# Moving the reciprocals of softmax sums from ScalarE's Ln and Exp to a power on GpSimd

## The chip, the cores and the metric

The kernel runs on one core of one Trainium2 chip. The metric is the time of one execution on the device, in microseconds (us); lower is better. Inside the core, PE (TensorE) does the matrix products, ACT (ScalarE), DVE (VectorE) and POOL (GpSimd) do elementwise work, SP issues DMAs. Each engine works through its own list of instructions in order and waits for semaphores where an instruction needs another engine's result.

## The reference

Attention with a softmax that has one more term in its denominator, followed by a feed-forward block with squared relu. There are 8 batches, 12 heads, 448 positions and a head dimension of 64; the block has 3584 tokens, width 768 and inner width 2048.

```python
def _attn_ref(q, k, v):
    scale = 1.0 / np.sqrt(q.shape[-1])
    scores = scale * np.matmul(q, k.transpose(0, 1, 3, 2))
    m = np.max(scores, axis=-1, keepdims=True)
    e = np.exp(scores - m)
    attn = e / (np.sum(e, axis=-1, keepdims=True) + np.exp(-m) + 1e-09)
    return np.matmul(attn, v)
# x = attention's output as [8 * 448, 12 * 64]
def _moe_ref(x, w_in, w_out):
    h = x @ w_in
    r = np.maximum(h, 0.0)
    return (r * r) @ w_out
```

Without the subtraction of the maximum the weights are exp(s) / (sum of exp(s) + 1). The kernel computes that form, so it needs one reciprocal of (sum + 1) for each query and head.

## The kernel before, in words

The twelve heads of a batch are worked on as three quads of four heads. Batches 1 to 7 give 21 quads, numbered m = 0 to 20 (three to a batch); batch 0 is worked on in halves by functions of its own and is not touched by the change. A quad goes through these steps, each a letter in a written-out list of steps:

- `s` (`quad_scores`): scores of 64 keys at a time into a PSUM tile `sp`; `e` (`quad_exp`, recorded at L254): ScalarE's exp of it, to a tile `et` or `nn`. There are seven of each to a quad.
- `a` (`add_quad`, L441 to L447): VectorE adds the exps of the seven pieces, in four instructions, to `half`.
- `S` (`sums_of_quad`): four matmuls with `ones`, whose entries are 1/256 (`GS` is 256), sum over the keys; each sum lands, already repeated over 64 rows, in a PSUM tile `zp`, of the kind `sp`.
- `Z` (`quad_z`, L463): ScalarE reads `zp` (128 x 896) and writes ln(sum/256 + 1/256) to an SBUF tile `rcp`; the 1/256 comes in as the bias `one_b`.
- `M` (`quad_reciprocal`, L466): ScalarE's exp(-x) in place, which is 256/(sum + 1).
- `v` (`values_step`): 28 matmuls of the exps with the values, into two PSUM tiles `mp`.
- `X` (`quad_x`, L487): two VectorE multiplies of `mp` and `rcp`, to the block's input `xt`.

The feed-forward block uses the letters `j` (matmuls with `win`), `k` (`relu`, L503 on ScalarE or L505 on VectorE), `l` (`squared`, L509, to `gs`), `o` (`out_piece`, matmuls with `wout`), `O` and `Q` (`out_first` and `out_second`, L575, L577 and L581, which evict the output; `store` then sends it from SP's queue). `d` issues loads: weights (`load_win`, `load_wout`), values (`load_v_quads`), staging of the queries and keys of later batches in DRAM (`stage`), transposed loads from there (on SP), and `tail_keys` (L188), copies by GpSimd that wait for those. All of GpSimd's loads and copies are in one queue.

The order is written by hand, as two strings, `ORDER` for the start and `CYCLE` for pairs of batches from the fourth on. Every engine's list follows that order, so a step that moves to another engine stands in that engine's list where its letter stands in the string. For instance, near the end of `ORDER`:

```
... Z7 Q12 a8,2 o13,12,16 v7,0 v7,1 v7,2 v7,3 O13,1 v7,4 a8,3 v7,5 v7,6 M7 S8 Q13 v8,0 v8,1 Z8 v8,2 v8,3 M8 v8,4 v8,5 X7 v8,6 X8
```

PSUM holds two `sp` tiles of two banks and, after the start, a ring of four `mp` tiles of one bank. Every `v`, `j` and `o` takes its tiles from that ring: a quad's values take two and give them back at `X`, a tile of the output takes two and gives them back at `Q`, a tile of the hidden layer takes one and gives it back at `k`. `z_pool` has two `rcp` tiles.

Of the kernel before, what the change touches and what calls it, by code (L numbers as in the profile page):

```python
# [9 lines left out]
FP32 = mybir.dt.float32  # L10
FP16 = mybir.dt.float16
AF = mybir.ActivationFunctionType
ALU = mybir.AluOpType
# [3 lines left out]
def kernel(  # L17
# [9 lines left out]
    nc = tc.nc  # L27

    B, H, S, D = q.shape
# [12 lines left out]
    scale = 1.0 / float(D) ** 0.5  # L42
    GS = 256.0
# [4 lines left out]
    consts = ctx.enter_context(tc.tile_pool(name="consts", bufs=1))  # L48
# [340 lines left out]
    eqs, esq, zqs = {}, {}, {}  # L389
# [70 lines left out]
    def quad_z(m):  # L460
        zp = zps.pop(m)
        rcp = zqs[m] = z_pool.tile([128, 2, S], FP32, name="rcp")
        nc.scalar.activation(out=rcp, in_=zp[:, :, 0:S], func=AF.Ln, bias=one_b)  # L463

    def quad_reciprocal(m):
        nc.scalar.activation(out=zqs[m], in_=zqs[m], func=AF.Exp, scale=-1.0)  # L466

    xqs = {}

# [120 lines left out]
    idle = nc.const_aps.tensor(1.0, [128, 512], mybir.dt.bfloat16)  # L590
    ones = consts.tile([128, 64], FP16)
    nc.vector.memset(ones, 1.0 / GS)
    one_b = consts.tile([128, 1], FP32)
    nc.vector.memset(one_b, 1.0 / GS)
    raw = load_first_quad()
# [38 lines left out]
    def quad_visit(n):  # L634
# [25 lines left out]
        "a": lambda m, step: add_quad(m, step),  # L660
        "S": lambda m: sums_of_quad(m),
        "Z": lambda m: quad_z(m),
        "M": lambda m: quad_reciprocal(m),
        "v": lambda m, c: values_step(m, c),
        "X": lambda m: quad_x(m),
# [46 lines left out]
    def period(b):  # L712
# [16 lines left out]
        def block(n):  # L729
# [5 lines left out]
            "a": lambda x, step: add_quad(m + x, step),  # L735
            "S": lambda x: sums_of_quad(m + x),
            "Z": lambda x: quad_z(m + x),
            "M": lambda x: quad_reciprocal(m + x),
            "v": lambda x, c: values_step(m + x, c),
            "X": lambda x: quad_x(m + x),  # L740
# [85 lines left out]
```

## Time and profile before

| | before |
|---|---|
| median of 2 runs | 392.89 us (391.95 to 393.84) |
| the profiled execution | 393.06 us |
| its span (first to last instruction) | 391.3 us |
| PE busy | 383.2 us, 98% |
| DVE busy | 251.9 us, 64% |
| ACT busy | 228.5 us, 58% |
| POOL busy | 62.2 us, 16% |

The profile is of one execution. Its span is 1.8 us shorter than the time of that execution; what lies around the span is not in any row. A row of a group gives the line, the engine, the operation, the tiles written and read, their shape, how many instructions there were, their busy time in us and the mean of one in ns, then the idle time of the engine just before them and what ended it. In a timeline a row begins with the start and the duration in us. GpSimd's spans in a profile are rough. The granted TensorE clock was 1.00 over all stages of this execution.

Three parts can be told apart in the order of time: up to about 47 us loads and batch 0; to 318 us attention and feed-forward work interleaved, with PE busy in nearly all of it (89.4 of 90 us from 47 to 137, and 45.0 of 45 from 183 to 228); after 318 us feed-forward work alone. The 21 logarithms of line L463 start between 47.8 and 314.3 us.

### The profile page before, as it was taken

The page shows a single profiled execution, that of the slowest core. Times are in us where ns is not written, and L with a number is a line of the kernel's source. Part 1 is how long each engine was busy: PE and PEld are TensorE (multiplying, and loading weights), DVE is VectorE, ACT ScalarE, POOL GpSimd, SP SyncE. Part 2 cuts the span into 40 slices and gives each one's busy share as a digit, 9 for nine tenths or more (in the row PEclk, how much of TensorE's full clock was granted, in tenths as well). Part 3 has the DMA queues.
Part 4 walks back from the last instruction along what each step waited for, and adds up shares of the span by engine and source line. Part 5 has one row for each costly group of instructions (what it writes and reads, how often), then busy time and mean ns, then how long its engine had stood idle before and what let it go on. Part 6 is the DMA issues. An engine that isn't in the chain of part 4 may idle for free.

```text
span 391.3 us, 14259 instructions
## 1 busy us (share of the span) xinstructions
PE 383.2 (98%) x6432; PEld 253.7 (65%) x6432; DVE 251.9 (64%) x468; ACT 228.5 (58%) x308; POOL 62.2 (16%) x96
## 2 busy tenths in 40 slices
PE   9789999999999999999999999999999999999997
PEld 5566656565789755667777665667777755556665
DVE  2887995765666766556968757566778788880000
ACT  5999998586689511349988731248988730001221
POOL 8544420025000701300001240310000000000000
PEclk9999999999999999999999999999999999999999
DMA  8999999999939899903129596941112200001132
GB/s 143 203 205 205 202 203 205 182 182 175 215 75 175 158 195 149 160 2 66 44 54 194 145 182 131 151 46 44 52 55 64 64 23 2 0 0 61 62 82 80
DMA packets 75052, 45.34 MB, mean 116 GB/s; under 512 B 47472, under 2 KB 72944, under 8 KB 74992
## 3 DMA queue, kind: packets, MB, share of 16 engines
q0 software_dynamic: 24752, 22.62, 37.4%
q1 hardware_dynamic: 49952, 21.59, 28.1%
q8 instruction: 50, 0.82, 0.9%
q10 hardware_dynamic: 288, 0.23, 0.2%
q14 instruction: 10, 0.08, 0.1%
HBM read 45.69 MB, written 17.93 MB: 163 GB/s over the span
## 4 chain that ended last, share of the span: by engine, by line
PE 86%; ACT 6%; DMA 2%; SPq 2%; DVE 1%; issue 1%; POOL 1%; ACTq 0%; POOLq 0%; DVEq 0%
PE mp L93 77%; PE sp L93 8%; ACT et L254 4%; SPq L166 2%; DMA nn<-in_k_dram 2%; PE mp L207 1%; DMA out_dram<-ot 1%; ACT rcp L372 1%; ACT nn L254 0%; DVE qk L217 0%; ACT rcp L365 0%; ACT ot L575 0%; DVE half L341 0%; ACT rcp L463 0%; DVE half L447 0%
## 5 line engine op out<-in xcount | busy, mean ns | idle before, releaser
L93 PE MATMUL mp<-wout,gs 64*64 64x384 f16 (+2 forms) x2928 | 165.2, 322 | 0.0
L93 PE MATMUL mp<-xt,win 128*64 128x448 f16 (+2 forms) x1188 | 148.3, 347 | 0.1
L93 PEld LDWEIGHTS <-gs 64*64 64x64 f16 (+1 forms) x2928 | 103.1, 106 | 34.5
L93 PEld LDWEIGHTS <-win 128*64 128x64 f16 (+1 forms) x1188 | 83.2, 106 | 63.5 <-issue 4.2
L254 ACT ACTIVATE et<-sp 128x896 f16<-128x896 f32 (+2 forms) x131 | 110.6, 889 | 12.3 <-PE sp L93 11.7
L505 DVE TENSOR_SCALAR rt<-mp 128x448 f16<-128x448 f32 x87 | 54.1, 622 | 17.4 <-PE mp L93 14.5
L509 DVE TENSOR_TENSOR gs<-rt 128x448 f16<-128x448 f16 x128 | 47.8, 390 | 22.1 <-ACT rt L503 20.2
L503 ACT ACTIVATE rt<-mp 128x448 f16<-128x448 f32 x41 | 21.8, 543 | 65.0 <-PE mp L93 55.7
L575 ACT ACTIVATE ot<-mp 128x384 f32<-128x384 f32 (+2 forms) x31 | 14.9, 480 | 71.6 <-PE mp L93 68.8
L93 PE MATMUL sp<-qk 64*64 64x224 f16 (+1 forms) x1056 | 53.7, 274 | 2.1 <-DVE qk L217 0.5
L93 PEld LDWEIGHTS <-qk 64*64 64x64 f16 x1056 | 32.7, 115 | 15.2 <-issue 6.5
L188 POOL COPY flatq<-qk 64x384 f16<-64x384 f16 x20 | 14.8, 739 | 172.7 <-DMA qk<-stage_k 126.0
L254 ACT ACTIVATE nn<-sp 128x896 f16<-128x896 f32 x42 | 37.1, 916 | 4.3 <-PE sp L93 4.2
L487 DVE TENSOR_TENSOR xt<-mp,rcp 128x448 f16<-128x448 f32 x42 | 24.2, 619 | 15.7 <-ACT rcp L466 10.3
L581 DVE SCALAR_TENSOR_TENSOR ot<-mp,ot 128x384 f32<-128x384 f32 x42 | 23.4, 556 | 15.3 <-ACT ot L575 12.4
L93 PEld LDWEIGHTS <-vn 64*64 64x64 f16 x756 | 22.4, 107 | 10.4 <-issue 1.8
L93 PE MATMUL mp<-et,vn 64*64 64x448 f16 (+1 forms) x448 | 24.5, 343 | 0.0
L577 DVE TENSOR_SCALAR ot<-mp 128x384 f32<-128x384 f32 x26 | 14.4, 555 | 14.3 <-PE mp L93 14.2
L463 ACT ACTIVATE rcp<-sp,one_b 128x896 f32<-128x896 f32 x21 | 21.1, 1007 | 2.8 <-PE sp L93 2.7
L466 ACT ACTIVATE rcp<-rcp 128x896 f32<-128x896 f32 x21 | 19.9, 949 | 0.5
L441 DVE TENSOR_TENSOR half<-et 128x1792 f16<-128x1792 f16 x15 | 16.3, 1088 | 4.3 <-ACT et L254 4.2
L443 DVE TENSOR_TENSOR half<-half,et 128x1792 f16<-128x1792 f16 x15 | 16.3, 1086 | 0.3
(59 smaller groups left out, 197.4 us busy)
## 6 DMA issues: line engine op xcount, KB each, us to landing
out_dram<-ot SPq DMA_DIRECT2D x52, 96.0 KB, 2.9
out_dram<-ot SPq DMA_DIRECT2D x19, 192.0 KB, 1.9
win<-in_moe_w_in_dram POOLq DMA_DIRECT2D x8, 384.0 KB, 12.3
wout<-in_moe_w_out_dram POOLq DMA_DIRECT2D x4, 768.0 KB, 14.9
vn<-in_v_dram POOLq DMA_DIRECT2D x10, 288.0 KB, 8.4
stage_q<-in_q_dram POOLq DMA_DIRECT2D x4, 676.0 KB, 13.1
stage_k<-in_k_dram POOLq DMA_DIRECT2D x4, 676.0 KB, 15.9
nn<-in_q_dram POOLq DMA_DIRECT2D x8, 224.0 KB, 8.6
```

The costliest lines, as they stand in the source:

```text
L93: return nc.tensor.matmul(out_, lhsT, rhs, start=start, stop=stop)
L254: nc.scalar.activation(out=out_, in_=in_, func=AF.Exp, scale=scale)
L441: nc.vector.tensor_add(esq[m], a[:, 0:w], a[:, w:2 * w])
L443: nc.vector.tensor_add(esq[m], esq[m], z[:, 0:w])
L463: nc.scalar.activation(out=rcp, in_=zp[:, :, 0:S], func=AF.Ln, bias=one_b)
L466: nc.scalar.activation(out=zqs[m], in_=zqs[m], func=AF.Exp, scale=-1.0)
L487: nc.vector.tensor_mul(xts[b][:, 2 * g + i, :], xqs[m][i][:, 0:S], zqs[m][:, i, :])
L503: nc.scalar.activation(out=rt[:, 0:m], in_=hp[:, 0:m], func=AF.Relu)
L505: nc.vector.tensor_scalar(out=rt[:, 0:m], in0=hp[:, 0:m], scalar1=0.0, scalar2=None, op0=ALU.max)
L509: nc.vector.tensor_mul(gs[:, f0:f0 + per, t0 % RING:t0 % RING + n], r, r)
L575: nc.scalar.activation(out=ot, in_=op[:, 0:w], func=AF.Copy, scale=OUT_SCALE)
L581: nc.vector.scalar_tensor_tensor(out=ot, in0=lo[:, 0:w], scalar=OUT_SCALE, in1=ot, op0=ALU.mult, op1=ALU.add)
```

## The change

For the quads of batches 1 to 7, `Z` becomes a VectorE addition of 1/256 that reads the sums from PSUM and writes them to `rcp`, and `M` becomes a GpSimd instruction with two tensors as inputs that raises `rcp` to the power of a tile `minus`, filled with -1 by GpSimd at the start. Batch 0 keeps ScalarE's Ln and Exp. The strings of the order are the same.

```diff
     def quad_z(m):
         zp = zps.pop(m)
         rcp = zqs[m] = z_pool.tile([128, 2, S], FP32, name="rcp")
-        nc.scalar.activation(out=rcp, in_=zp[:, :, 0:S], func=AF.Ln, bias=one_b)
+        nc.vector.tensor_scalar(out=rcp, in0=zp[:, :, 0:S], scalar1=1.0 / GS, scalar2=None, op0=ALU.add)
 
     def quad_reciprocal(m):
-        nc.scalar.activation(out=zqs[m], in_=zqs[m], func=AF.Exp, scale=-1.0)
+        nc.gpsimd.tensor_tensor(out=zqs[m], in0=zqs[m], in1=minus, op=ALU.pow)
...
     ones = consts.tile([128, 64], FP16)
     nc.vector.memset(ones, 1.0 / GS)
+    minus = consts.tile([128, 2, S], FP32)
+    nc.gpsimd.memset(minus, -1.0)
     one_b = consts.tile([128, 1], FP32)
```

In the built program the 21 additions stand in VectorE's list and the 21 powers in GpSimd's. The memset of `minus` (128 x 896) stands in GpSimd's list ahead of its first loads. The powers of quads 0 to 2 stand between loads of values and of `wout` and the first staging loads, that of quad 3 behind the four copies of batch 3's `tail_keys`.

## What was predicted

> **What bounds the kernel now.** I read the page first: busy times, then the chain that ended last.
>
> ```profile
> span 391.3 us, 14259 instructions
> PE 383.2 (98%) x6432; PEld 253.7 (65%) x6432; DVE 251.9 (64%) x468; ACT 228.5 (58%) x308; POOL 62.2 (16%) x96
> PE 86%; ACT 6%; DMA 2%; SPq 2%; DVE 1%; issue 1%; POOL 1%; ACTq 0%; POOLq 0%; DVEq 0%
> ```
>
> PE is busy for 383.2 of 391.3 us and makes up 86% of the chain. Only 8.1 us of PE idle time exist, so relieving ScalarE, here or anywhere, can win at most 2%; whatever makes PE wait is paid in full. The question is therefore how late the normalized rows (`xt`) come, and how long PE can go on without them.
>
> Then the groups by line, for the instructions that the change touches or that I price it by:
>
> ```profile
> L463 ACT ACTIVATE rcp<-sp,one_b 128x896 f32<-128x896 f32 x21 | 21.1, 1007 | 2.8 <-PE sp L93 2.7
> L466 ACT ACTIVATE rcp<-rcp 128x896 f32<-128x896 f32 x21 | 19.9, 949 | 0.5
> L487 DVE TENSOR_TENSOR xt<-mp,rcp 128x448 f16<-128x448 f32 x42 | 24.2, 619 | 15.7 <-ACT rcp L466 10.3 <-PE sp L93 3.8 <-PE mp L93 1.7
> L505 DVE TENSOR_SCALAR rt<-mp 128x448 f16<-128x448 f32 x87 | 54.1, 622 | 17.4 <-PE mp L93 14.5
> L577 DVE TENSOR_SCALAR ot<-mp 128x384 f32<-128x384 f32 x26 | 14.4, 555 | 14.3 <-PE mp L93 14.2
> masks.py:199 POOL TENSOR_SCALAR_AFFINE_SELECT ident<-ident 128x128 f16<-128x128 f16 x1 | 0.3, 288 | 0.1
> ```
>
> The 21 logarithms (L463) and 21 exponentials (L466) take 1.007 and 0.949 us each. The multiply that uses them (L487) already waits for them, 10.3 us in all, without cost to PE: there is some cover, but it has been tested over about 1 us at a time only.
>
> Then the timeline of ScalarE, VectorE and GpSimd around single quads (start, duration):
>
> ```profile
> 80.45 1.00 ACT L463 ACTIVATE rcp<-sp,one_b 128x896 f32<-128x896 f32 x1
> 81.48 0.95 ACT L466 ACTIVATE rcp<-rcp 128x896 f32<-128x896 f32 x1
> 82.46 1.16 DVE L487 TENSOR_TENSOR xt<-mp,rcp 128x448 f16<-128x448 f32 x2 [2.00 <-ACT rcp L466]
> ...
> 82.02 1.29 POOL L188 COPY flatq<-qk 64x384 f16<-64x384 f16 x2 [30.35 <-DMA qk<-stage_k]
> 86.31 1.82 POOL L188 COPY flatq<-qk 64x384 f16<-64x384 f16 x2 [3.01 <-DMA qk<-stage_k]
> ```
>
> From the start of the logarithm to the multiply are 2.01 us; in 12 of the 21 quads it is 2.0 to 2.1. GpSimd, which now gets the second step, spends its queue waiting for transposed loads there: these copies stand ahead of this quad's power in program order.
>
> **The change part by part.** ScalarE loses 42 instructions, 41.0 us; by the 8.1 us above this is worth little. On the one stretch where they are on the chain (116.43 to 118.12 us) they are 1.67 us; I count this gain as nothing and keep it for a rival.
>
> VectorE gains 21 additions of 128x896 from PSUM. L577 and L505 give 555 ns for 384 columns and 622 for 448, that is 1.05 ns a column, so 622 + 448 x 1.05 = 1.09 us, against 1.007 on ScalarE.
>
> GpSimd gains 21 powers of 128x896 f32. No row shows a power. Its nearest row of price is the select above, 288 ns for 128 columns, 2.25 ns a column: one simple pass over 896 is 2.0 us, the lower bound. A power of two tensors is a logarithm, a product and an exponential; if each is a polynomial with its splitting and scaling, I estimate 16 steps, and a pass of 2.0 us for each step gives 32 us, the upper bound. Steps in one loop needn't load and store each time, yet sixteen can't be free as in a table: I take the geometric middle, 8.0 us, and keep both ends.
>
> The Trainium skill's GPSIMD Engine Reference, section 3.1, has bodies of more than two operations run at about 3 operations a cycle of 1.2 GHz; with some 48 operations that is an estimate of 12 us, and the sum below would end near 618. No run here shows that rule.
>
> Now the delay of one quad. Addition 1.09, power 8.0, one more handover 0.1, less the 2.02 of before: the multiply can start 7.17 us later. VectorE is in order, and the multiply waits at the head of it: relu (L505), squares (L509), sums of exps (L441 to L447) and the output's evictions (L577, L581) queue behind it, and PE waits for these, since the ring of PSUM tiles holds four and the values of the quad keep two until the multiply.
> - 21 quads: 21 x 7.17 = 150.6.
> - Five quads (7/8, 10/11, 13/14, 16/17, 19/20 as pairs) issue the second addition ahead of the first multiply. There the second multiply follows the first after one power, 8.0, where it now follows after 2.1: it adds 5.9, not 7.17. 5 x -1.27 = -6.4.
> - Queue of GpSimd: the copies end at 88.13 (86.31 + 1.82) where the addition would end at 81.54: +6.6 for quad 3. The copies at 222.22 + 1.52 = 223.74 stand ahead of quad 12's power, ready at 218.15: +5.6. Together 12.2. The weight and staging loads behind the first three powers move by some us each; the first use of the second half of `wout` is near 81 us against a landing at 67 to 77, so I count nothing, and if that cover is gone the loads cost what the powers ahead of them do, which is in the 7.17 already.
> - The memset of 128x896 on GpSimd ahead of its first loads, which open the chain: between 0.1 (a 128x1 memset) and 2.0 (the pass above); I take 1.0.
> - Cover: behind the values PE has one output tile that needs no VectorE, 64 matmuls of 64x384; 32 of them take 1.30 us in the chain, so 2.6. VectorE must afterwards catch up two multiplies and an eviction, 2 x 0.62 + 0.56 = 1.8. That leaves 0.8 a quad: -16.8.
>
> Sum: 150.6 - 6.4 + 12.2 + 1.0 - 16.8 = +140.6. The profiled execution took 393.06 (span 391.3 and 1.8 around it), 0.2 above the median 392.89. 393.06 + 140.6 = 533.7, say 534.
>
> **The rivals.**
> Cheap power. At 2.0 us the delay of a quad is 1.17: 24.6 - 6.4 + 12.2 + 1.0 - 16.8 = +14.6, 408; without cover, because VectorE is 70 to 90% busy in those slices, 424. For it: every GpSimd row is near 2 ns a column. Against: none of them computes a function.
> Dear power. At 32 us: delay 31.17; 654.6 - 6.4 + 12.2 + 1.0 - 16.8 = +644.6, 1038. For it: nothing but the step count; against: steps in registers cost less than passes.
> Port. A power that reads SBUF holds off VectorE's additions of two SBUF tensors, so one L441 (1.08 us) of each quad that now runs before the multiply starts after the power: 21 x 1.08 = 22.7, 534 + 22.7 = 556. For it, by the groups of single lines:
>
> ```profile
> L188 POOL COPY flatq<-qk x20: 609/624/1360, 82.0 to 258.7; 64x384 f16<-64x384 f16 x20
> L509 DVE TENSOR_TENSOR gs<-rt x128: 376/391/601, 30.4 to 352.7; 128x448 f16<-128x448 f16 x128
> ```
>
> The same copy takes 609 to 1360 ns and the same square 376 to 601; something holds them. Against: in a quad that waits for the power VectorE has little else to do. The Trainium skill's SBUF page (SBUF — State Buffer, section "SBUF: two separate sides") calls the pair of ports that VectorE and GpSimd share an exclusive lock for a whole instruction; the longest copies here agree with it.
> Not slower. If the power took under 1.6 us (0.83 that the new steps may cost, and the 0.8 of cover), as the fastest copy's 609 ns for 384 columns, 1.4 us for 896, would allow, every multiply would come in time. ScalarE's exps, freed of 1.67 us on the chain, would repay the memset, and with the copies (12.2) hidden by PE's order the time would be 393.06 - 1.67 + 1.0 = 392.4. Against: the 12.2 has no visible cover, and the copy has one input and no arithmetic.
> That GpSimd does not get the work is excluded: in the built order 21 powers stand on its queue and 21 additions on VectorE's.
>
> **How the numbers follow.** Forecast, a power of about 4 to 16 us without further loss: 0.45. Cheap 0.22, dear 0.18, port 0.08, not slower 0.07. The range runs from the cheap power with a short memset (393.06 + 13.7 = 407, taken as 405) to the dear one (1038, taken as 1040); outside lie the last rival and a power slower than the passes. Within 2% (385 to 401, about what a measurement of this kernel tells from no change) is the last rival and nearly nothing else, 0.07; faster by more than 2% would need all of PE's idle time, 0.01; slower 0.92.
>
> **What would show each step.** Right: a group on POOL of 21 instructions near 8 us; VectorE's waits headed by the multiply for GpSimd's `rcp`, near 21 x 6 us; PE's share of the span near 72% (383 of 532); the power of quad 3 held by the copies. ScalarE's busy time near 188. Wrong: a power near 2 us with PE over 90% (cheap), or one so long that its 21 durations alone exceed the span of before (dear). The mean duration of the power decides nearly everything: each us of it is worth 21 us of time, as long as it is over about 2.

## The result, and the profile after

| | before | after |
|---|---|---|
| median | 392.89 us | 3399.48 us (3399.32 to 3399.63, 2 runs) |
| ratio to before | | 8.65 (95% interval 8.56 to 8.74) |
| span of the profiled execution | 391.3 us | 3397.5 us |
| mean granted TensorE clock | 1.00 | 0.562 |

Predicted were 534 us, with a range of 405 to 1040. The direction was right and the size was far off. Medians are of runs in the faster of two states; one of the four runs of e9 below (533.1 us) fell in the slower one and is left out.

The page of the kernel after, its busy times, two rows of its 40 slices, and its chain:

```profile
span 3397.5 us, 14261 instructions
PE 445.0 (13%) x6432; PEld 300.9 (9%) x6432; DVE 1091.2 (32%) x489; ACT 192.0 (6%) x266; POOL 3074.3 (90%) x118
POOL 6999989898989999859999799999499997999991
PEclk8555555556555555575555655555855555555559
POOL 80%; PE 8%; POOLq 6%; issue 4%; DVE 1%; ACT 1%; DMA 0%; SPq 0%; DVEq 0%; ACTq 0%
```

The engine that was busy for 16% of the span is now busy for 90% of it, and it is the chain. The 6% of POOLq and most of the 4% of issue belong to it too: those pieces (202 us from 3120, 52 us from 1234, 58 us from 2176) lie inside powers that were running. PE, the bound before, is at 13%. Its clock is granted at about half in most slices; in the trace the stretches at 0.5 lie in PE's waits for the powers (from 1300 to 1428 us, a wait throughout, the mean is 0.50; from 1467 to 1480, with PE busy throughout, it is 1.00).

The groups that made it so:

```profile
L466 POOL TENSOR_TENSOR rcp<-rcp,minus 128x896 f32<-128x896 f32 x21 | 3010.8, 143377 | 169.4 <-DVE rcp L463 169.2
L487 DVE TENSOR_TENSOR xt<-mp,rcp 128x448 f16<-128x448 f32 x42 | 24.3, 620 | 2164.7 <-POOL rcp L466 2164.7
L445 DVE TENSOR_TENSOR half<-half 128x896 f16<-128x896 f16 x21 | 95.4, 4543 | 0.2
```

One power of 128 x 896 takes 143.4 us, 160.0 ns a column. The 21 of them take 3010.8 us, and the time rose by 3006.6: nearly the whole result stands in one row. That the two agree so closely is partly chance, since other terms of either sign, some tens of us, lie between them (see the last sections). VectorE's multiply, which waited 10.3 us for its reciprocals before, now waits 2164.7. The third row is odd: a plain addition in fp16, 0.6 us before, has a mean of 4.5 us (see below).

The waits, in total, times, longest:

```profile
PE mp L93 <- DVE xt L487: 2391.9, 20, 145.2
DVE xt L487 <- POOL rcp L466: 2164.7, 21, 146.4
POOL rcp L466 <- DVE rcp L463: 169.2, 14, 47.8
```

PE waits for the multiply, the multiply for the power, and the power hardly for anything: 169 us in all. Read from bottom to top this is the prediction's chain.

The addition that replaced the logarithm took 1080 to 1092 ns (1.09 us was predicted), and ScalarE's busy time fell to 192.0 us ("near 188"). The memset of `minus` took 0.846 us, but the first load behind it was issued only 0.28 us later than before (1.53 against 1.25 us), where the prediction took 1.0.

### The profile page after: what moved, and what is told of

Its sections match the earlier page's. It is cut to its first block, busy times and chain, and to the rows that moved or that the text cites. A ratio compares the mean times of both kernels' runs of the same rounds, so it can differ in the third digit from the quotient of the medians.

```text
span 3397.5 us, 14261 instructions
## 1 busy us (share of the span) xinstructions
PE 445.0 (13%) x6432; PEld 300.9 (9%) x6432; DVE 1091.2 (32%) x489; ACT 192.0 (6%) x266; POOL 3074.3 (90%) x118
## 4 chain that ended last, share of the span: by engine, by line
POOL 80%; PE 8%; POOLq 6%; issue 4%; DVE 1%; ACT 1%; DMA 0%; SPq 0%; DVEq 0%; ACTq 0%
POOL rcp L466 79%; PE mp L93 7%; POOLq L823 6%; PE sp L93 1%; DVE rcp L463 0%; DVE xt L487 0%; ACT et L254 0%; DMA nn<-in_k_dram 0%; DMA qk<-stage_k 0%; POOL flatq L188 0%; PE mp L207 0%; DVE ot L577 0%; ACT nn L254 0%; ACT rcp L372 0%; DVE half L447 0%
## 5 line engine op out<-in xcount | busy, mean ns | idle before, releaser
L466 POOL TENSOR_TENSOR rcp<-rcp,minus 128x896 f32<-128x896 f32 x21 | 3010.8, 143377 | 169.4 <-DVE rcp L463 169.2
L487 DVE TENSOR_TENSOR xt<-mp,rcp 128x448 f16<-128x448 f32 x42 | 24.3, 620 | 2164.7 <-POOL rcp L466 2164.7
L93 PE MATMUL mp<-wout,gs 64*64 64x384 f16 (+2 forms) x2928 | 191.6, 350 | 1095.1 <-DVE xt L487 1092.8
L447 DVE TENSOR_TENSOR half<-half,nn 128x896 f16<-128x896 f16 x6 | 332.1, 55349 | 0.3
L93 PE MATMUL mp<-xt,win 128*64 128x448 f16 (+2 forms) x1188 | 165.4, 372 | 871.7 <-DVE xt L487 871.2
L93 PEld LDWEIGHTS <-gs 64*64 64x64 f16 (+1 forms) x2928 | 128.9, 115 | 1137.1 <-issue 987.0
L441 DVE TENSOR_TENSOR half<-et 128x1792 f16<-128x1792 f16 x15 | 180.6, 12040 | 5.5 <-ACT et L254 5.5
L93 PEld LDWEIGHTS <-win 128*64 128x64 f16 (+1 forms) x1188 | 98.5, 112 | 938.2 <-issue 829.9
L443 DVE TENSOR_TENSOR half<-half,et 128x1792 f16<-128x1792 f16 x15 | 179.9, 11996 | 0.3
L445 DVE TENSOR_TENSOR half<-half 128x896 f16<-128x896 f16 x21 | 95.4, 4543 | 0.2
L443 DVE TENSOR_TENSOR half<-half,nn 128x1792 f16<-128x1792 f16 x6 | 88.3, 14724 | 1.1 <-ACT nn L254 1.0
## 6 DMA issues: line engine op xcount, KB each, us to landing
out_dram<-ot SPq DMA_DIRECT2D x19, 192.0 KB, 1.9
```

What stands on the lines that cost most here:

```text
L93: return nc.tensor.matmul(out_, lhsT, rhs, start=start, stop=stop)
L441: nc.vector.tensor_add(esq[m], a[:, 0:w], a[:, w:2 * w])
L443: nc.vector.tensor_add(esq[m], esq[m], z[:, 0:w])
L445: nc.vector.tensor_add(esq[m][:, 0:2 * S], esq[m][:, 0:2 * S], esq[m][:, 2 * S:w])
L447: nc.vector.tensor_add(esq[m][:, 0:2 * S], esq[m][:, 0:2 * S], z[:, w:w + 2 * S])
L466: nc.gpsimd.tensor_tensor(out=zqs[m], in0=zqs[m], in1=minus, op=ALU.pow)
```

## The experiments

All diffs are against the kernel after, unless another is named. In several of them the reciprocal is left out; the expectations say where. Times are medians; the ratio to the kernel before, on the same chip, has its 95% interval where there were three rounds.

**A product, and four products, in place of the power.**

```diff
-        nc.gpsimd.tensor_tensor(out=zqs[m], in0=zqs[m], in1=minus, op=ALU.pow)
+        nc.gpsimd.tensor_tensor(out=zqs[m], in0=zqs[m], in1=minus, op=ALU.mult)   # e1; e2: four times
```

e1, one product:

> GpSimd multiplies the sums by the tile of -1 in place of the power; the reciprocal is left out. Everything else is as after the change. Theory A (the sum of the prediction is right in its structure, and only the price of the power was wrong): the time follows 365.5 + 21 P, with P the measured mean of the GpSimd instruction, for P of 2 us or more; at P = 2.0 that is 408 us, at 4.0 it is 450. Theory B (the sum came near at the long power only because large terms hide small ones; each quad also loses VectorE's held additions, about 1.1 us, and PE's slower clock after a wait): 20 us or more above A's line, at least 430 at P = 2.0. Theory C (the loss is not in the length of the power but in the move itself, its place in the queue of GpSimd): hundreds of us even here.

e2, four products:

> Four such products one after the other in place of the power, the reciprocal left out: GpSimd's step is some 8 us long, the price that the prediction took. Theory A: 365.5 + 21 P with P the length of the four together, 534 us at P = 8.0. Theory B: 20 us or more above that line, with VectorE's additions of two SBUF tensors held up by GpSimd and PE's granted clock under 1. Theory C: about the time of e1, since the number of places in the queue is the same.

The group on GpSimd in e1, and in e2:

```profile
L466 POOL TENSOR_TENSOR rcp<-rcp,minus 128x896 f32<-128x896 f32 x21 | 45.6, 2174 | 159.6 <-DVE rcp L463 159.4
```

```profile
L467 POOL TENSOR_TENSOR rcp<-rcp,minus 128x896 f32<-128x896 f32 x84 | 181.2, 2160 | 168.0 <-DVE rcp L463 162.8
```

e1 took 445.8 us (ratio 1.133, 1.128 to 1.138), e2 576.6 us (1.466, 1.460 to 1.472). With P of 2.17 and 4 x 2.16 = 8.64 us, A's line gives 411 and 547: both are over it, by 35 and 30 us. Theory C is out, since e2 costs 131 us more than e1 for 6.46 us more of P: 20.2 us for each us, against the 21 of the sum. The slope is A's, the offset is B's; which part of B is left to the runs below. The product of the same shape, form and place is 66 times cheaper than the power, so the price is that of the function and not of two tensors on GpSimd.

**What the price of the power hangs on.** Half of the columns (e3), eight rows (e4), another exponent (e7).

```diff
+        nc.gpsimd.tensor_tensor(out=zqs[m][:, 0], in0=zqs[m][:, 0], in1=minus[:, 0], op=ALU.pow)   # e3
+        nc.scalar.activation(out=zqs[m][:, 1], in_=zqs[m][:, 1], func=AF.Ln)
+        nc.scalar.activation(out=zqs[m][:, 1], in_=zqs[m][:, 1], func=AF.Exp, scale=-1.0)
...
+        nc.gpsimd.tensor_tensor(out=zqs[m][0:8], in0=zqs[m][0:8], in1=minus[0:8], op=ALU.pow)   # e4
...
+    nc.gpsimd.memset(minus, 1.0)   # e7
```

e3:

> The power for half of the columns (128 x 448); ScalarE takes Ln and Exp of the other half. Theory A (a fixed price per column, 160 ns): the power takes 71.7 us and the time is 365.5 + 21 x 71.7 = 1871 us. Rival (a large fixed part per instruction, such as code that is loaded for each power): the power takes clearly more than 72 us, up to 143, and the time more than 1900 us.

e4:

> The power on rows 0 to 7 alone, all 896 columns; the reciprocal of the other rows is left out. Theory 1 (the elements of a column within a group of 16 rows are taken one after the other): the power takes half, 72 us, and the time is near 1870 us. Theory 2 (a column of all rows is one step, long in itself): 143 us as after the change, and a time near 3380 to 3400 us.

e7:

> The change with an exponent of +1 in place of -1; the reciprocal is left out. Theory 1 (one general routine for every exponent): the power takes 143.3 us as after the change, and the time is 3380 to 3400 us. Theory 2 (the price hangs on the exponent, with a short way for simple ones): clearly less, and the time is 389 + 21 P by the line through e3 and the kernel after.

The groups of e3, e4 and e7, one from each:

```profile
L466 POOL TENSOR_TENSOR rcp<-rcp,minus 128x448 f32<-128x448 f32 x21 | 1512.3, 72020 | 171.2 <-DVE rcp L463 171.0
```

```profile
L466 POOL TENSOR_TENSOR rcp<-rcp,minus 8x896 f32<-8x896 f32 x21 | 3010.6, 143367 | 171.0 <-DVE rcp L463 170.8
```

```profile
L466 POOL TENSOR_TENSOR rcp<-rcp,minus 128x896 f32<-128x896 f32 x21 | 3010.8, 143377 | 169.4 <-DVE rcp L463 169.2
```

The times were 1902.5, 3398.9 and 3401.1 us (one run each). Half of the columns cost half: 160.8 ns a column against 160.0, so there is next to no fixed part, and e3's rival is out by the duration. The time of e3 is over A's figure of 1871, though: the line gives 365.5 + 21 x 72.02 = 1878, and the remaining 25 us are an offset as in e1 and e2. Eight rows cost what 128 do: a column is one step for all rows, theory 2 of e4. An exponent of +1 costs what -1 does: theory 1 of e7, no short way for this exponent. What GpSimd does in those 160 ns no run shows, nor whether the price hangs on the values that are raised, or would differ with a constant exponent in place of the tile.

**VectorE's addition alone (e8).** ScalarE takes Ln and Exp of the sum that VectorE has written; nothing is on GpSimd but the memset.

```diff
-        nc.gpsimd.tensor_tensor(out=zqs[m], in0=zqs[m], in1=minus, op=ALU.pow)
+        nc.scalar.activation(out=zqs[m], in_=zqs[m], func=AF.Ln)
+        nc.scalar.activation(out=zqs[m], in_=zqs[m], func=AF.Exp, scale=-1.0)
```

> One part of the change alone: VectorE adds the offset, then ScalarE takes Ln and Exp of the sum, as long together (1.96 us) as GpSimd's product in e1 (2.17). The memset stays. Theory Q (what e1 lost above the line of the prediction comes from GpSimd: its queue, in which loads and copies wait, and the port that it shares with VectorE): the time is near the prediction's sum without the copies, 393 + 21 x 1.19 - 6 - 17 + 1, 396 us, at most 405. Theory X (it comes from the later multiply and VectorE's longer list, whichever engine does the second step): 425 us or more, near e1.

414.1 us (1.054, 1.049 to 1.059): neither theory. It is 18 us over theory Q and 11 us under X. By the starts in the traces, from the last matmul of the sums to the multiply took 3.20 us in the mean of the 21 quads before, and 4.47 us in e8: 21 x 1.27 = 26.7 us later, of which the time shows 21.3. By this difference PE had about 5.4 us in hand and not the 16.8 of the prediction, 0.26 us a quad instead of 0.8; no run took the cover by itself. The rest of the 18 us lies mostly in the lateness: the expectation had 21 x 1.19 - 6 = 19 us of it, 8 less than the trace. With GpSimd's step gone an offset of half the size of e1's 35 us remains, so not all of that need come from GpSimd. The page of e8:

```profile
PE 391.3 (95%) x6432; PEld 271.9 (66%) x6432; DVE 272.9 (66%) x489; ACT 228.3 (55%) x308; POOL 62.3 (15%) x97
PE 70%; DVE 11%; ACT 10%; issue 3%; DMA 2%; SPq 2%; POOL 1%; DVEq 0%; POOLq 0%; ACTq 0%
```

VectorE is idle for a third of the span and stands on the chain for 11%, where it was 1% before: an engine's mean load does not tell whether one more instruction on it comes in time.

**The copies behind the GpSimd step (e10).** As e1, with the order's letters for tail copies (and the loads of batch 4's values) moved.

```diff
- ... S3 Z3 v3,0 d25 v3,1 v3,2 v3,3 ... M3 o1,0,4
+ ... S3 Z3 v3,0 v3,1 v3,2 v3,3 ... M3 d25 o1,0,4
- ... d29 ... d30 ... M7 ... M8 v8,4
+ ... M7 ... M8 d29 d30 v8,4
- ... d12 ... d11 ... M3 ... M4 ... M5 v5,3
+ ... M3 ... M4 ... M5 d12 d11 v5,3
```

> e1 (a product in place of the power, the reciprocal left out) with the tail copies of batches 3, 4 and 6, and the loads of batch 4's values, put behind the GpSimd step of the quads that they stood ahead of (quads 3, 7, 8, 12 to 14). Theory Q1 (the queue of GpSimd: quads 3 and 12 wait for copies): PE's waits of 5.7 us at 92 us and 4.1 us at 257 us of e1 go, and the time falls from 446 by about 10, to 436 us. Theory Q2 (the port and the halved clock after waits make the offset): within 3 us of 446.

432.8 us (1.100, 1.096 to 1.103): 13.0 us less than e1. Theory Q1. The timeline of GpSimd around quad 3 in e1, then in e10:

```profile
89.47 1.28 POOL L188 COPY flatq<-qk 64x384 f16<-64x384 f16 x2 [17.38 <-DMA qk<-stage_k]
93.48 1.27 POOL L188 COPY flatq<-qk 64x384 f16<-64x384 f16 x2 [2.72 <-DMA qk<-stage_k]
94.83 2.06 POOL L466 TENSOR_TENSOR rcp<-rcp,minus 128x896 f32<-128x896 f32 x1
```

```profile
89.50 2.08 POOL L466 TENSOR_TENSOR rcp<-rcp,minus 128x896 f32<-128x896 f32 x1 [16.58 <-DVE rcp L463]
91.53 1.29 POOL L188 COPY flatq<-qk 64x384 f16<-64x384 f16 x2
```

The step that waited for transposed keys it does not need starts 5.3 us earlier. From the start of VectorE's addition to that of the multiply quad 3 took 10.6 us in e1 and takes 3.4 here, quad 12 8.9 and 4.9. The prediction had 6.6 and 5.6, together 12.2 us, for these two. Quads 7 and 8, which the edit moved too and for which it had nothing, gained 3.6 and 2.8 us.

**A step that reads nothing (e11).** Against e10, three memsets in place of the product.

```diff
-        nc.gpsimd.tensor_tensor(out=zqs[m], in0=zqs[m], in1=minus, op=ALU.mult)
+        for _ in range(3):
+            nc.gpsimd.memset(zqs[m], 0.5)
```

> e10 with three memsets of rcp (constant 0.5) in place of the product: GpSimd's step is about as long (3 x 0.85 = 2.5 us against 2.17), in the same place of its queue, but reads nothing; the reciprocal is left out. By the line through the kernels, 21 us for each us, it would be 21 x 0.38 = 8 us slower than e10, 441 us. Theory P (the 14 us by which e10 lies above e8 and their difference in length are VectorE's additions of two SBUF tensors, held while GpSimd reads): VectorE's additions take no longer than 1.1 us beside the memsets, and the time is about 441 - 14 = 427 us, below e10. Theory N (the 14 us are one more handover, or PE's clock after waits): 438 to 444 us.

423.6 us (1.078, 1.074 to 1.081), below e10 although its step is longer: theory P. The step in e10, and then one of the three memsets in e11:

```profile
L466 POOL TENSOR_TENSOR rcp<-rcp,minus 128x896 f32<-128x896 f32 x21 | 46.4, 2208 | 206.3 <-DVE rcp L463 206.3
```

```profile
L467 POOL MEMSET rcp<- 128x896 f32 x63 | 53.2, 844 | 191.3 <-DVE rcp L463 188.9
```

That is 2.21 us against 3 x 0.844 = 2.53. VectorE's first addition of exps (line L441, ns: least, median, most), in e10 and then in e11:

```profile
L441 DVE TENSOR_TENSOR half<-et x15: 1079/1092/2809, 39.2 to 333.5; 128x1792 f16<-128x1792 f16 x15
```

```profile
L441 DVE TENSOR_TENSOR half<-et x15: 1080/1083/1094, 39.5 to 328.0; 128x1792 f16<-128x1792 f16 x15
```

Beside GpSimd's product, which reads SBUF, the addition of two SBUF tensors takes up to 2.81 us: it ended 0.95 us after the product did, nearly its own 1.08. Beside memsets it takes its own time alone. VectorE's busy time, 287.3 us in e10 and 270.4 in e11, gives the holds of all lines together: 17 us.

**The power in two halves (e12).** This asks what the held additions cost in the kernel after, where they are 30 times longer. One timeline of that kernel, VectorE, then GpSimd, then PE:

```profile
1142.16 0.55 DVE L581 SCALAR_TENSOR_TENSOR ot<-mp,ot 128x384 f32<-128x384 f32 x1
1142.62 82.78 DVE L445 TENSOR_TENSOR half<-half 128x896 f16<-128x896 f16 x1
1225.51 0.63 DVE L447 TENSOR_TENSOR half<-half,nn 128x896 f16<-128x896 f16 x1
...
1142.39 286.56 POOL L466 TENSOR_TENSOR rcp<-rcp,minus 128x896 f32<-128x896 f32 x2 [6.93 <-DVE rcp L463]
...
1226.19 0.59 PE L93 MATMUL sp<-half,ones 64*64 64x448 f16 x4 [81.55 <-DVE half L447]
```

```diff
-        nc.gpsimd.tensor_tensor(out=zqs[m], in0=zqs[m], in1=minus, op=ALU.pow)
+        for i in range(2):
+            nc.gpsimd.tensor_tensor(out=zqs[m][:, i], in0=zqs[m][:, i], in1=minus[:, i], op=ALU.pow)
```

> The change with each power issued as two powers of 128x448, one after the other. The 21 pairs take 21 x 144 us as before. In the kernel after, VectorE's additions that fell into a power were held for 82 us; beside the powers of 448 columns of e3 they were held about 1 us. Theory 1 (the holds cost nothing, because the multiply waits 143 us in any case): the additions are held once or twice for some 1 us, or up to one half power (72 us), and the time stays 3400 us, plus 21 handovers and the little that 160.8 ns a column are above 160.0 (21 x 0.7 = 14): 3400 to 3420. Theory 2 (the holds are part of the chain): the time falls by more than 50 us.

3404.1 us: theory 1. That addition by its line (least, median, most in ns), in the kernel after and then in e12:

```profile
L445 DVE TENSOR_TENSOR half<-half x21: 609/617/82779, 42.0 to 3034.8; 128x896 f16<-128x896 f16 x21
```

```profile
L445 DVE TENSOR_TENSOR half<-half x21: 609/616/1386, 42.4 to 3038.6; 128x896 f16<-128x896 f16 x21
```

The 82 us holds are gone, VectorE's busy time falls from 1091.2 to 280.4 us, and the time is 4.6 us longer. The two halves together were 11.1 us longer (3021.9 against 3010.8 for all quads), so by this one run the holds can hardly have cost more than some 10 us in all: next to nothing beside 143 us of power in each quad. The edit changed one more thing: the first of the two multiplies starts after the first half already, 73 us after the start of VectorE's addition for that quad in place of 144.6. That did not bring time either.

**VectorE's reciprocal (e9)**, as another way to take the work from ScalarE.

```diff
-        nc.gpsimd.tensor_tensor(out=zqs[m], in0=zqs[m], in1=minus, op=ALU.pow)
+        nc.vector.reciprocal(zqs[m], zqs[m])
```

> VectorE takes the reciprocal itself after its addition; nothing is on GpSimd but the memset. No row shows a reciprocal on VectorE. If it runs at one column a cycle like the addition (1.1 us), the step Z to X is as long as before, 2.0 us, and VectorE gets 44 us more work where it is 64% busy: 393 to 400 us. If it is iterated eight times (some 8 us), 21 x 7 us stand in VectorE's own list and the time is about 393 + 21 x 7 - 17 = 523 us.

The group, and PE's longest waits:

```profile
L466 DVE RECIPROCAL rcp<-rcp 128x896 f32<-128x896 f32 x21 | 120.7, 5746 | 0.2
```

```profile
PE mp L93 <- DVE xt L487: 63.0, 20, 6.5
PE mp L93 <- DVE ot L581: 15.6, 3, 5.3
```

5.75 us each, 6.4 ns a column, and 525.0 us (1.339, 1.329 to 1.348; 524.4 to 531.0 in three runs). That is 46 us more than the expectation's own formula gives at 5.75 us (393 + 21 x 4.92 - 17 = 479). PE's waits for the evictions (the second row; before, 0.2 us in all for that pair) suggest why: a step on VectorE itself also holds up what could have passed it while another engine computed. No run separates this.

No kernel tried here beats the one before.

## Why the prediction was wrong

**The step that failed: the price of the power.** It took 8.0 us, between a simple pass of 2.0 and sixteen passes of 32; the measured mean is 143.4. The lower bound held (a product is 2.17 us). The upper bound was none: it assumed that a step of a polynomial costs at most one pass over the tile, and that there are sixteen, and neither was in any row. The power costs as much as 66 products. With it, the 21 x 135.4 = 2843 us that were missing are in the sum: 533.7 + 2843 = 3377, against 3399.5 measured. The rival "dear" was right in kind, and its price was under a quarter of the true one; the sentence "one so long that its 21 durations alone exceed the span of before" is what came: 3011 against 391.

The estimate by the Trainium skill's GPSIMD Engine Reference, section 3.1 (about 3 operations a cycle) was 12 us, a twelfth of what was measured. By the page's rate and its 1.2 GHz, 160.0 ns would be 192 cycles and 576 operations a column (an estimate), where the prediction assumed 48. Whether the rate or the count was off no run shows.

**The rest of the sum, term by term.**
- Slope: 21 us for each us of the step. From e1 to e2 it is 20.2, from e3 to the kernel after (3399.5 - 1902.5) / (143.38 - 72.02) = 20.98. Right.
- Addition 1.09: 1.08. Right.
- Memset 1.0: it delayed the opening loads by 0.3. Too large, and small.
- Copies ahead in GpSimd's queue, 12.2: 13.0 by e10, all moved copies and loads together. Right in kind; that the sizes agree so well is partly luck, since quads 7 and 8 are in the 13.0 and not in the 12.2. And the loads behind the powers were counted as nothing, and in e1 they show: the staging of batch 5 is issued at 137.05 us behind the step of quad 6, where it was at 91.75 before; it then runs beside the transposed loads of batch 4, the first of which takes 11.4 us where it took 4.2 before, and PE waits 6.5 us once for an output tile that is not yet stored. This was read from the traces and not tried by itself.
- Cover 16.8: about 5.4 by the difference in e8. Too large by 11.
- Port: written as a rival at 23 us. The holds are real (e11). In short steps they cost: e10 to e11 is -9.2 us, where the 0.32 us more of step would be +7, so 16 us (an estimate; VectorE's busy time differs by 17); in the kernel after they hardly cost more than some 10 us in all (e12). As a rival of the forecast at 8 us it may have had some truth: e2, at 8.64 us, came out at 576.6 where the sum gives 547, but how much of these 30 us are holds no run shows.

**The cheap rival, as it would have been.** With a GpSimd step of 2.17 us the change would still have been 13% slower (e1), not the 4 to 8% of the rival. The direction did not hang on the price: every version tried was slower, the mildest (e8) by 5%. The offset of e1 can be put together from parts: 411 by the prediction's line, 11 for the cover that was not there, 16 for the held additions and 6.5 for the late staging make 445, against 445.8 measured. So close a match is luck. The 8 us by which the multiplies of e8 came later than its formula are left out, the parts come from different kernels, and PE's clock is in several of them: the clock record of e1 has 24 us at half clock, which is up to 12 us of PE's work (an estimate). How e1's offset divides stays open; that of the kernel after, 23 us, is under 1% of its loss.

**Not slower** was rightly small: PE was at 98%, and no version tried shows a gain from what was taken from ScalarE.

## What to carry to other kernels

A function on an engine that has never been seen to compute one has no upper bound from rows of other operations; run it once, alone, before it is put on 21 places of a chain. Where one engine is at 98%, work taken from another can win almost nothing, while each step of a chain of results that gets longer is paid nearly in full, times the number of passes (here 20 to 21 us for each us, in 21 passes): look for the first consumer in order, and at what stands ahead of the moved step in its new queue. The structure of a sum can be checked apart from its prices, by a cheap operation of the same form in the same place.

## What the runs showed of the hardware

- A power of two tensors on GpSimd costs 160 ns a column, linear in columns (72.0 us for 448, 143.4 for 896), the same for 8 rows and 128, and for exponents +1 and -1. A product of the same form costs 2.4 ns a column (2.17 us for 896).
- An addition of two SBUF tensors on VectorE, issued during a power of 896 columns, ended 82.95 to 84.2 us after the power's start, not at its end at 143.3. Beside a power of 448 columns (e3, e12) such additions were held for 0.8 us at most. Taking off an addition's own time, the release is some 82.4 us after the start, the time of 515 columns at 160.0 ns (an estimate); what sets it no run shows. The Trainium skill's SBUF page (SBUF — State Buffer, section "SBUF: two separate sides") has the pair of ports held for the full instruction; for the product and the copies that agrees, for the power the hold ended after 57% of it.
- Memsets on GpSimd did not hold such additions (e11), as that section says of instructions that do not read.
- The granted clock was 0.562 in the mean of the kernel after and 0.863 in that of e2. In e1 PE's waits of 2.9, 5.7, 6.5 and 4.1 us (from 62, 92, 153 and 257 us) are followed by stretches at half clock of 3.4, 6.8, 6.8 and 6.8 us (from 65, 95, 157 and 263 us); a wait of 2.4 us at 364 is not. PE's busy time for the same 6432 matmuls was 383.2 us before, 401.6 in e1 and 445.0 in the kernel after. How much of the 23 to 35 us that the sums leave open is due to the clock, no run separates.
